# Retention followed by a feed-forward block: another activation, and the second product one chunk behind the first

## The chip, the cores and the metric

The kernel runs on one core of a Trainium2 chip. The time is that of the device for one execution, in microseconds; lower is better.

## What is computed

q, k and v are [8, 8, 576, 64] in float32, w_in [512, 2048] and w_out [2048, 512] in float64.

```python
scores = scale * np.matmul(q, k.transpose(0, 1, 3, 2))
ret = scores * Dmat[None, :, :, :]        # gamma_h ** (i - j) where j <= i, else 0
attn = np.matmul(ret, v)
x = np.ascontiguousarray(attn.transpose(0, 2, 1, 3)).reshape(B * S, H * D)   # [4608, 512]
h = x @ w_in
sp = np.maximum(h, 0.0) + np.log1p(np.exp(-np.abs(h)))                       # softplus
g = h * erf(sp)
out = (g @ w_out).astype(np.float32)
```

## The kernel before

**Retention.** The sequences are cut into 40 pieces of up to 128 tokens of one batch element with all heads (per batch element four of 128 tokens and one of 64). `piece_stages` is a generator with three stages for a piece, written in this order on every engine's queue: the transposes of q and k into PSUM and their copies `qT`, `kT` to SBUF (L222, L224); the scores of the two heads of each pair and their causal mask `sT` (L232, L235); the outputs from `sT` and v, from qT and the running `state`, the product `kv` for the next state, the evacuation of the outputs into `xT` and the state's update (L247 to L291). All PSUM tiles of these stages come from one pool of two buffers, `at`. `load` fetches a piece two ahead, on SP's queue; POOL scales the keys (L208).

**Weights.** They come in float64 and are rounded to float32 on the chip, in 32 parts of 512 weights per partition, two of w_in and two of w_out for a group. `round_weights(g)` does a group's four parts: two ACT operations (L166, L167), five on DVE (L169 to L181), two on POOL (L185, L186), on temporaries `wa`, `wb`, `wr` with two buffers each.

**Feed-forward.** The 4608 tokens are nine chunks of 512, and d_ff is eight groups of two blocks of 128: 72 slots (c, g). A slot's first product (`hidden`, L323) makes `ph`, one PSUM tile per block, which ACT copies to `h` in SBUF (L330). `softplus_terms`, `softplus` and `serf` make g from h: Softplus through Tanh, Abs and Ln, Erf through Gelu and a reciprocal, with a power series for small values, on ACT, DVE and POOL. The second product (`project`, L379) of the group runs two slots later (`LAG`), in four PSUM tiles `po` that collect a chunk's eight groups; ACT copies them out (L388).

**Order.** The schedule is manual: instructions stand on each engine in the order of the program. Four pieces of retention come first, each followed by the four parts of one group; then the loop over slots, in which a slot's two halves of the second product alternate with stages of the retention for the next chunk, and slots 0 to 3 of the first chunk end with four parts of weights each:

```python
        for part in range(2):
            if i >= LAG:
                project(*slots[i - LAG], range(part * NTT // 2, (part + 1) * NTT // 2))
            if now:
                base, goal = stages_for((c + 1) * TCH), stages_for((c + 2) * TCH)
                attend(base + (goal - base) * (2 * g + 1 + part) // (2 * n_g))
```

Of the kernel before, what the change touches and what calls it, by code (L numbers as in the profile page):

```python
# [52 lines left out]
def kernel(  # L53
# [67 lines left out]
    def weight_parts(g):  # L121
# [7 lines left out]
        for ft in range(g * GF, (g + 1) * GF):  # L129
            yield w_out_sb[:, ft : ft + 1, :], w_out[ft * P : (ft + 1) * P, :].rearrange(  # L130
                "(c p) f -> p c f", p=P
            ), slice(0, D_MODEL)

    parts = [(g, *part) for g in range(n_g) for part in weight_parts(g)]
# [311 lines left out]
```

## Time and profile before

| | |
|---|---|
| time, median of 3 runs | 1539.33 us (1535.58 to 1543.75) |
| profiled execution, first to last instruction | 1537.4 us; its time around that is not listed apart, and the median is 1.9 us above the span |
| busy share of the span | DVE 85%, PE 83%, POOL 68%, PE's weight loads 43%, ACT 56% |
| mean granted clock of TensorE | 0.907 of full |
| HBM traffic | 45.68 MB read, 9.44 MB written, 36 GB/s over the span |

A line of a timeline gives the start in us from the first instruction, the duration, the engine, the line of the kernel and the operation, the tiles as output<-input, shapes, how many instructions were merged (x16), and in brackets the idle time of the engine before it with what ended it. The first product's 1152 matmuls are those of two instructions for each matmul of the source. The granted clock is a share of the full 2.4 GHz; the lower level is 0.5. "Busy" of PE is the union of its instructions, so a matmul that runs at the lower clock counts as longer busy.

### The profile page before, as it was taken

Reading aid. Unit: us, or ns where it says so; the run is one execution under the profiler, and the core shown is the slowest. Engines: PE = TensorE matmul, PEld = TensorE weight load, DVE = VectorE, ACT = ScalarE, POOL = GpSimd, SP = SyncE. Lnnn points to the kernel's source line nnn. Section 1 sums busy time; section 2 is a strip of 40 time slices with the busy share of each in tenths; the row PEclk is TensorE's granted clock in tenths of the full one; section 3 lists DMA queues with packets and bytes.
Section 4 is the critical chain, followed back from the end, with each engine's and each line's share of the span. In section 5 each row is a group of like instructions: output and inputs, shape, how many; then the busy total and the mean of one; then the engine's idle time right before and its main releaser. Section 6 shows DMA issues by size and latency. Waiting matters only on the chain.

```text
span 1537.4 us, 12085 instructions
## 1 busy us (share of the span) xinstructions
PE 1281.9 (83%) x4416; PEld 662.0 (43%) x4416; DVE 1299.4 (85%) x853; ACT 858.3 (56%) x893; POOL 1039.7 (68%) x542
## 2 busy tenths in 40 slices
PE   3451454999999899998998999989999999989885
PEld 3330222554444455544444454444444444444332
DVE  5678999887888879888888888898898988888884
ACT  2126443466665556665665666555656665557762
POOL 3346566667776677757766677767777767666774
PEclk7566777999999899999999999999999999999997
DMA  7233220021101210120101110110111110000000
GB/s 191 73 110 89 75 75 14 11 42 48 21 11 21 62 27 12 21 62 8 21 11 48 41 22 29 30 35 9 47 31 35 28 38 1 0 0 27 1 0 28
DMA packets 124556, 55.91 MB, mean 36 GB/s; under 512 B 113616, under 2 KB 113616, under 8 KB 124496
## 3 DMA queue, kind: packets, MB, share of 16 engines
q1 hardware_dynamic: 124352, 54.54, 14.0%
q8 instruction: 35, 0.57, 0.1%
q10 hardware_dynamic: 144, 0.59, 0.1%
q14 instruction: 25, 0.20, 0.0%
HBM read 45.68 MB, written 9.44 MB: 36 GB/s over the span
## 4 chain that ended last, share of the span: by engine, by line
DVE 50%; PE 26%; ACT 16%; issue 5%; POOL 3%; DMA 0%; POOLq 0%; DVEq 0%; ACTq 0%
DVE r L361 18%; PE ph L323 12%; DVE s L353 6%; DVE r L363 6%; DVE r L367 4%; PE o L247 3%; DVE wa L175 3%; PE o L257 3%; DVE wa L172 3%; PE po L379 2%; DVE r L364 2%; PE kv L283 2%; ACT L343 2%; ACT L360 2%; DVE sT L235 2%
## 5 line engine op out<-in xcount | busy, mean ns | idle before, releaser
L379 PE MATMUL po<-w_out_sb,h 128*128 128x512 f32 x1152 | 525.9, 604 | 24.5 <-POOL h L368 24.5
L323 PE MATMUL ph<-xT,w_in_sb 128*128 128x512 f32 x1152 | 525.5, 610 | 6.0 <-ACT h L330 5.4
L361 DVE RECIPROCAL r<-s 128x1024 f32<-128x1024 f32 x72 | 471.8, 6553 | 7.0
L368 POOL TENSOR_TENSOR h<-h,r 128x1024 f32<-128x1024 f32 x72 | 169.7, 2357 | 357.4 <-DVE r L367 325.5
L379 PEld LDWEIGHTS po<-w_out_sb,h 128*128 128x128 f32 x1152 | 218.1, 193 | 290.6 <-issue 256.2
L323 PEld LDWEIGHTS ph<-xT,w_in_sb 128*128 128x128 f32 x1152 | 221.0, 197 | 262.8 <-issue 255.6
L330 ACT COPY h<-ph 128x512 f32<-128x512 f32 x144 | 83.1, 585 | 398.3 <-PE ph L323 398.3
L353 DVE SCALAR_TENSOR_TENSOR s<-h,s 128x1024 f32<-128x1024 f32 x72 | 167.9, 2332 | 49.7 <-ACT s L343 49.7
L346 POOL TENSOR_TENSOR tail<-tail,p 128x1024 f32<-128x1024 f32 x72 | 185.3, 2574 | 6.0
L349 POOL TENSOR_TENSOR tail<-tail,p 128x1024 f32<-128x1024 f32 x72 | 181.5, 2520 | 5.6
L348 POOL TENSOR_TENSOR tail<-tail,p 128x1024 f32<-128x1024 f32 x72 | 177.4, 2463 | 6.0
L247 PE MATMUL o<-sT,raw_v 128*64 128x128 f32 (+1 forms) x640 | 68.3, 327 | 114.2 <-DVE sT L235 113.8
L363 DVE TENSOR_TENSOR r<-r,z 128x1024 f32<-128x1024 f32 x72 | 131.5, 1827 | 8.6 <-ACT z L360 8.6
L232 PE MATMUL s<-qT,kT 64*128 64x128 f32 (+1 forms) x640 | 70.0, 294 | 82.0 <-DVE kT L224 82.0
L166 ACT ACTIVATE wa<-wraw 128x512 f32<-128x512 f32 x32 | 21.5, 672 | 171.3 <-POOL w_in_sb L186 142.4
L247 PEld LDWEIGHTS o<-sT,raw_v 128*64 128x64 f32 (+1 forms) x640 | 49.5, 171 | 151.0 <-DVE sT L235 144.6
L232 PEld LDWEIGHTS s<-qT,kT 64*128 64x128 f32 (+1 forms) x640 | 62.2, 196 | 111.0 <-DVE kT L224 89.8
L339 ACT ACTIVATE p<-h 128x1024 f32<-128x1024 f32 x72 | 76.1, 1057 | 59.0 <-POOL tail L349 58.4
L272 DVE TENSOR_TENSOR xT<-o,cst 128x512 f32<-128x512 f32 (+1 forms) x44 | 25.7, 591 | 90.9 <-PE o L257 82.9
L367 DVE COPY_PREDICATED r<-mask,tail 128x1024 f32<-128x1024 uint8 x72 | 94.7, 1315 | 7.8 <-DVE r L364 0.9
L347 POOL TENSOR_SCALAR tail<-tail 128x1024 f32<-128x1024 f32 x72 | 95.6, 1327 | 6.3
L185 POOL TENSOR_TENSOR wb<-wb,wr 128x512 f32<-128x512 f32 x32 | 41.6, 1301 | 86.0 <-DVE wb L181 86.0
(43 smaller groups left out, 1587.7 us busy)
## 6 DMA issues: line engine op xcount, KB each, us to landing
out_dram<-osb SPq DMA_DIRECT2D x36, 256.0 KB, 2.1
raw_k<-in_k_dram SPq DMA_DIRECT2D x32, 256.0 KB, 3.1
raw_q<-in_q_dram SPq DMA_DIRECT2D x32, 256.0 KB, 4.0
raw_v<-in_v_dram SPq DMA_DIRECT2D x32, 256.0 KB, 4.3
wraw<-in_moe_w_in_dram SPq DMA_DIRECT2D x16, 512.0 KB, 3.4
wraw<-in_moe_w_out_dram SPq DMA_DIRECT2D x16, 512.0 KB, 3.3
raw_k<-in_k_dram SPq DMA_DIRECT2D x8, 128.0 KB, 2.9
raw_q<-in_q_dram SPq DMA_DIRECT2D x8, 128.0 KB, 3.5
```

The source lines that it names most:

```text
L232: nc.tensor.matmul(ps[:n, p, :n], lhsT=T["k"][r, p, :n], rhs=T["q"][r, p, :n], start=True, stop=True)
L247: nc.tensor.matmul(o[e * D : (e + 1) * D, p, :n], lhsT=t["v"][:n, 2 * p + e, :], rhs=sT[:n, e, p, :n], start=(p == 0), stop=(old is None a ...
L323: nc.tensor.matmul(ph, lhsT=w_in_sb[:, dc, f : f + P], rhs=xts[c][:, dc, :], start=(dc == 0), stop=(dc == n_dc - 1),)
L346: nc.gpsimd.tensor_tensor(out=e, in0=e, in1=p2, op=ALU.mult)
L348: nc.gpsimd.tensor_tensor(out=e, in0=e, in1=p2, op=ALU.mult)
L349: nc.gpsimd.tensor_tensor(out=e, in0=e, in1=p, op=ALU.add)
L353: nc.vector.scalar_tensor_tensor(out=s, in0=h, scalar=1e-30, in1=s, op0=ALU.max, op1=ALU.subtract)
L361: nc.vector.reciprocal(out=r, in_=s)
L363: nc.vector.tensor_tensor(out=r, in0=r, in1=z, op=ALU.mult)
L367: nc.vector.copy_predicated(r, m, tail)
L368: nc.gpsimd.tensor_tensor(out=h, in0=h, in1=r, op=ALU.mult)
L379: nc.tensor.matmul(po[tt], lhsT=h[:, j * TCH + tt * P : j * TCH + (tt + 1) * P], rhs=w_out_sb[:, ft, :], start=(ft == 0), stop=(ft == n_ft ...
```

## The change

- *Activation.* `ph` is one PSUM tile of 1024 columns (two buffers) for both blocks. ACT writes Softplus of it to SBUF and then Erf in place, and DVE multiplies by `ph`, read from PSUM. The temporaries, the power series, the reciprocal and POOL's share go, as does the copy of h.
- *Second product one chunk behind.* In chunk c, slot g, the loop has four quarters: first product of block 0, second product, first product of block 1, second product. The second products are those of chunk c - 1, in the order `steps_out`: all eight groups for the first two blocks of 128 tokens, then all eight for the other two. `gpool` has 12 buffers, so that a chunk's eight g stay; the raw weights share them. After the last chunk, eight slots hold second products alone.
- *Staged retention.* The three stages are functions, listed so that a piece's transposes stand between the scores and the outputs of the piece before; a quarter ends with at most one stage. Scores alternate the two heads, each in its own PSUM tile. The copies `qT`, `kT` move from DVE to ACT.
- *Weights.* All of w_in is rounded before w_out, in place: the destination serves as `wa`, the raw words as `wb` and `wr`. Four parts stand ahead of the first slot, one at a time among the stages; the other 28 at the ends of slots 1 to 7 of chunk 0, four each. Four parts are fetched ahead instead of three.

```diff
-    WAHEAD = 3
-    LAG = 2  # slots between a group's first product and its second
+    WAHEAD = 4
...
-    raw = ctx.enter_context(tc.tile_pool(name="raw", bufs=PREFETCH + 1))
+    raw = ctx.enter_context(tc.tile_pool(name="raw", bufs=PREFETCH + 2))
...
-    gpool = ctx.enter_context(tc.tile_pool(name="gpool", bufs=LAG + 2))
...
+    gpool = ctx.enter_context(tc.tile_pool(name="gpool", bufs=12))
...
+    parts = [p for g in range(n_g) for p in parts_in(g)] + [p for g in range(n_g) for p in parts_out(g)]
+    N_IN = len(parts) // 2
...
+                t_f = gpool.tile([P, W], FP32, tag="g", name="wraw")
...
+            r_f, high_f = pairs_f[:, :, :, 0], pairs_f[:, :, :, 1]
+            a_f, a = dst, dst.bitcast(UINT32)
             nc.scalar.activation(a_f, high_f, AF.Abs)
             nc.scalar.mul(out=r_f, in_=low, mul=2.0**-52)
...
+            nc.vector.tensor_scalar(out=high, in0=a, scalar1=0xFF800000, scalar2=None, op0=ALU.bitwise_and)
+            nc.gpsimd.tensor_tensor(out=r_f, in0=high_f, in1=r_f, op=ALU.mult)
+            nc.gpsimd.tensor_tensor(out=a_f, in0=a_f, in1=r_f, op=ALU.add)
             load_weights()
...
-            T[name] = att.tile([P, NP, P], FP32, tag=name + "T", name=name + "T")
-            nc.vector.tensor_copy(out=T[name][:, :, :n], in_=pt[:, :, :n])
...
+            t[name + "T"] = att.tile([P, NP, P], FP32, tag=name + "T", name=name + "T")
+            nc.scalar.copy(out=t[name + "T"][:, :, :n], in_=pt[:, :, :n])
...
+    def scores(i):
+        n, t = pieces[i][2], live[i]
+        sT = t["sT"] = att.tile([P, 2, NP, P], FP32, tag="sT", name="sT")
+        ps = [ps_at.tile([P, NP, P], FP32, tag="at", name=f"s{e}") for e in range(2)]
+        for p in range(NP):
+            for e in range(2):
+                r = slice(e * D, (e + 1) * D)
+                nc.tensor.matmul(
+                    ps[e][:n, p, :n], lhsT=t["kT"][r, p, :n], rhs=t["qT"][r, p, :n], start=True, stop=True
+                )
...
+    stages = [(transposes, 0)]
+    for i in range(len(pieces)):
+        stages.append((scores, i))
+        if i + 1 < len(pieces):
+            stages.append((transposes, i + 1))
+        stages.append((outputs, i))
...
+    def serf(c, g, ph):
+        t = gs_of[c, g] = gpool.tile([P, W], FP32, tag="g", name="g")
+        nc.scalar.activation(t, ph, AF.Softplus)
+        nc.scalar.activation(t, t, AF.Erf)
+        nc.vector.tensor_tensor(out=t, in0=ph, in1=t, op=ALU.mult)
...
+    steps_out = [(half, g) for half in range(2) for g in range(n_g)]
...
+    need = stages_for(TCH)
+    for n in range(need):
+        attend(n + 1)
+        round_weights(1 + (N_IN // n_g + 1) * (n + 1) // need)
+    QUARTERS = 4
+    for c in range(n_ch + 1):
+        for g in range(n_g):
+            if c < n_ch:
+                ph = ps_h.tile([P, W], FP32, tag="ph", name="ph")
+                base, goal = stages_for((c + 1) * TCH), stages_for(min((c + 2) * TCH, n_tok))
+            for part in range(QUARTERS):
+                if c < n_ch and part % 2 == 0:
+                    hidden(c, g, [part // 2], ph)
+                    if part == 2:
+                        serf(c, g, ph)
+                elif c > 0 and part % 2 == 1:
+                    project(c - 1, 2 * g + part // 2)
+                if c < n_ch:
+                    attend(base + (goal - base) * (QUARTERS * g + part + 1) // (QUARTERS * n_g))
+            if c == 0:
+                round_weights(N_IN // n_g * (g + 2) + N_IN * g // n_g)
+            if c == 1:
+                round_weights(len(parts))
```

PE in a slot of the main loop, before (`ph` is the first product, `po` the second, `pt` transposes, `s` scores):

```order
L323 MATMUL ph<-xT,w_in_sb 128x512 x8
L379 MATMUL po_834<-w_out_sb,h 128x512 x2
L379 MATMUL po_837<-w_out_sb,h 128x512 x2
L232 MATMUL s_1363<-qT,kT 128x128 x4
L232 MATMUL s_1369<-qT,kT 128x128 x4
L379 MATMUL po_861<-w_out_sb,h 128x512 x2
L379 MATMUL po_864<-w_out_sb,h 128x512 x2
L247 MATMUL o<-sT,raw_v 64x128 x8
```

and PE in a slot of chunk 1 of the changed kernel:

```order
L308 MATMUL ph<-xT,w_in_sb 128x512 x4
L334 MATMUL po_1078<-w_out_sb,g 128x512 x2
L334 MATMUL po_1081<-w_out_sb,g 128x512 x2
L205 MATMUL pt_q<-ident,raw_q 128x128 x4
L205 MATMUL pt_k<-ident,raw_k 128x128 x4
L308 MATMUL ph<-xT,w_in_sb 128x512 x4
L334 MATMUL po_1078<-w_out_sb,g 128x512 x2
L334 MATMUL po_1081<-w_out_sb,g 128x512 x2
L234 MATMUL o<-sT,raw_v 64x128 x8
L270 MATMUL kv<-raw_v,raw_k 128x128 x4
```

The first product is cut in two and the second lies between; where scores and outputs stood one half of a second product apart, stages now stand two groups apart or more.

DVE from the end of slot 2's rounding to slot 3's in chunk 0 of the changed kernel (`g<-ph,g` is the multiply, L159 to L170 a part of the rounding):

```order
L170 TENSOR_SCALAR wraw<-w_in_sb 128x512
L259 TENSOR_TENSOR xT<-o,cst 128x4x128
L275 TENSOR_TENSOR state<-kv,cst 128x512
L320 TENSOR_TENSOR g<-ph,g 128x1024
L220 TENSOR_TENSOR sT<-s_640,cst 128x512
L220 TENSOR_TENSOR sT<-s_641,cst 128x512
L159 TENSOR_SCALAR w_in_sb<-w_in_sb 128x2x256
L162 TENSOR_SCALAR w_in_sb<-w_in_sb 128x2x256
```

The evacuations that free `at` and `ph` stand behind a whole burst of four parts; before, they stood behind the reciprocal as well.

ACT at slot 7 of chunk 0 of the changed kernel, with the waits (Pool, DVE, PE and DMAHW name the engine or DMA queue waited for):

```order
L156 ACTIVATE w_out_sb<-wraw 128x512 [waits DMAHW5_49]
L157 ACTIVATE wraw<-wraw 128x512
L207 COPY qT<-pt_q 128x4x64 [waits PE_49]
L207 COPY kT<-pt_k 128x4x64 [waits PE_49]
L318 ACT_TABLE_LOAD [waits DVE_49,PE_49]
L318 ACTIVATE g<-ph 128x1024 [waits Pool_49]
L319 ACT_TABLE_LOAD
L319 ACTIVATE g<-g 128x1024 [waits Activation_49]
```

Softplus writes to a buffer that raw weights had, and so waits for POOL's last read of them; in slot 7 this is the last part of slot 6's burst.

## Rows read from the trace of the kernel before

**Rows 1.** The page: busy us (share of the span) and instructions by engine.

```profile
PE 1281.9 (83%) x4416; PEld 662.0 (43%) x4416; DVE 1299.4 (85%) x853; ACT 858.3 (56%) x893; POOL 1039.7 (68%) x542
```

**Rows 2.** The page: the chain that ended last, shares by engine.

```profile
DVE 50%; PE 26%; ACT 16%; issue 5%; POOL 3%; DMA 0%; POOLq 0%; DVEq 0%; ACTq 0%
```

**Rows 3.** Windows: stretch, length, busy by engine, granted clock, DMA share, GB/s.

```profile
0.00:99.30 99.30, 40.56 (x216) 35.02 (x217) 61.42 (x86) 18.51 (x29) 37.08 (x35) 0.64 0.49 129
99.30:274.50 175.20, 81.53 (x283) 43.37 (x282) 158.25 (x142) 73.76 (x89) 109.45 (x69) 0.71 0.22 65
274.50:1523.20 1248.70, 1149.65 (x3906) 579.58 (x3904) 1079.68 (x625) 763.65 (x771) 893.12 (x439) 0.96 0.10 25
```

**Rows 4.** Timeline of PE in two slots of the main stretch.

```profile
1110.97 7.03 PE L323 MATMUL ph<-xT,w_in_sb 128*128 128x512 f32 x16
1117.84 3.60 PE L379 MATMUL po<-w_out_sb,h 128*128 128x512 f32 x8
1121.27 0.60 PE L222 MATMUL pt_q<-ident,raw_q 128*128 128x128 f32 x4
...
1122.15 3.60 PE L379 MATMUL po<-w_out_sb,h 128*128 128x512 f32 x8
1127.13 1.71 PE L232 MATMUL s<-qT,kT 64*128 64x128 f32 x16 [1.39 <-DVE kT L224]
1128.78 7.13 PE L323 MATMUL ph<-xT,w_in_sb 128*128 128x512 f32 x16
...
1139.27 1.09 PE L247 MATMUL o<-sT,raw_v 128*64 128x128 f32 x16
1140.30 1.16 PE L257 MATMUL o<-qT,state 128*128 128x128 f32 x8
1141.29 1.06 PE L283 MATMUL kv<-raw_v,raw_k 128*128 128x128 f32 x8
1142.18 3.60 PE L379 MATMUL po<-w_out_sb,h 128*128 128x512 f32 x8
```

**Rows 5.** Groups by line on ACT: busy us, mean ns, idle before.

```profile
L339 ACT ACT_TABLE_LOAD x72 | 92.4, 1283 | 1.3
L330 ACT COPY h<-ph 128x512 f32<-128x512 f32 x144 | 83.1, 585 | 398.3 <-PE ph L323 398.3
L360 ACT ACTIVATE z<-s 128x1024 f32<-128x1024 f32 x72 | 76.1, 1057 | 0.9
L166 ACT ACTIVATE wa<-wraw 128x512 f32<-128x512 f32 x32 | 21.5, 672 | 171.3 <-POOL w_in_sb L186 142.4 <-POOL w_out_sb L186 18.3 <-DMA wraw<-in_moe_w_in_dram 10.4
```

**Rows 6.** Groups by line on DVE: the state's add, with kv in PSUM.

```profile
L290 DVE TENSOR_TENSOR state<-kv,state 128x512 f32<-128x512 f32 x24 | 16.6, 690 | 9.1 <-PE kv L283 8.7
```

**Rows 7.** Timeline of PE near the end, after a gap.

```profile
1473.88 8.83 PE L379 MATMUL po<-w_out_sb,h 128*128 128x512 f32 x16 [2.48 <-POOL h L368]
```

**Rows 8.** Timeline of ACT at the end: the last copy of the output.

```profile
1533.72 0.60 ACT L388 ACTIVATE osb<-po 128x512 f32<-128x512 f32 x1 [1.40 <-PE po L379]
```

**Rows 9.** Timeline of DVE and POOL in the second burst of rounding.

```profile
45.75 0.42 DVE L169 TENSOR_SCALAR wa<-wa 128x512 f32<-128x512 f32 x1
...
48.42 1.31 POOL L185 TENSOR_TENSOR wb<-wb,wr 128x512 f32<-128x512 f32 x1 [11.11 <-DVE wb L181]
48.65 1.37 DVE L172 TENSOR_SCALAR wa<-wa 128x512 uint32<-128x512 uint32 x1
...
50.05 1.63 DVE L175 SCALAR_TENSOR_TENSOR wa<-wraw,wa 128x512 uint32<-128x512 uint32 x1
...
60.83 0.43 DVE L181 TENSOR_SCALAR wb<-wa 128x512 uint32<-128x512 uint32 x1
```

**Rows 10.** Timeline of PE before the first slot: the scores of two pieces.

```profile
62.51 3.09 PE L232 MATMUL s<-qT,kT 64*128 64x128 f32 x16 [16.63 <-DVE kT L224]
...
90.14 3.09 PE L232 MATMUL s<-qT,kT 64*128 64x128 f32 x16 [16.63 <-DVE kT L224]
```

**Rows 11.** Windows, the second product's instructions alone, main stretch.

```profile
274.50:1523.20 1248.70, 494.07 (x1088) 205.21 (x1088) 0.96 0.10 25
```

More of the change, by code (lines that the diff above doesn't have):

```diff
@@ L106, in load @@
         loaded[i] = t
-    for i in range(PREFETCH):
-        load(i)
+    load(0)
     cst = const.tile([P, CONST_COLS], FP32, name="cst")
@@ L116, with parts_in, parts_out @@
     tri = cst[:, H + 2 * NP * P : CONST_COLS]
+    for i in range(1, PREFETCH):
+        load(i)
     w_in_sb = const.tile([P, n_dc, D_FF], FP32, name="w_in_sb")
     w_out_sb = const.tile([P, n_ft, D_MODEL], FP32, name="w_out_sb")
-    def weight_parts(g):
+    def parts_in(g):
         f = g * GF * P
-        for dc in range(0, n_dc, WP // (GF * P)):
-            dcs = slice(dc, dc + WP // (GF * P))
-            yield w_in_sb[:, dcs, f : f + GF * P], w_in[dcs.start * P : dcs.stop * P, :].rearrange(
-                "(c p) f -> p c f", p=P
-            ), slice(f, f + GF * P)
+        step = WP // (GF * P)
+        for dc in range(0, n_dc, step):
+            src = w_in[dc * P : (dc + step) * P, :].rearrange("(c p) f -> p c f", p=P)
+            yield w_in_sb[:, dc : dc + step, f : f + GF * P], src, slice(f, f + GF * P)
+    def parts_out(g):
         for ft in range(g * GF, (g + 1) * GF):
[L130 to L134, printed above, removed]
+            src = w_out[ft * P : (ft + 1) * P, :].rearrange("(c p) f -> p c f", p=P)
+            yield w_out_sb[:, ft : ft + 1, :], src, slice(0, D_MODEL)
+    parts = [p for g in range(n_g) for p in parts_in(g)] + [p for g in range(n_g) for p in parts_out(g)]
+    N_IN = len(parts) // 2
     words = []
+    rounded = [0]
     def load_weights():
         if len(words) < len(parts):
-            _, dst, src, cols = parts[len(words)]
+            dst, src, cols = parts[len(words)]
             t = None
@@ L193 @@
     make_identity(nc, ident)
-    half = const.tile([P, 1], FP32, name="half")
-    nc.vector.memset(half, 0.5)
     xts = {}
+    live = {}
     state = {"prev": None}
@@ L210, in weigh_keys, with transposes @@
             )
-    def piece_stages(i):
-        b, s0, n = pieces[i]
-        t = loaded.pop(i)
+    def transposes(i):
+        n = pieces[i][2]
+        t = live[i] = loaded.pop(i)
         load(i + PREFETCH)
         weigh_keys(i + 1)
-        T = {}
         for name in "qk":
@@ L240, in piece_stages, with outputs @@
             )
-        yield
+    def outputs(i):
+        b, s0, n = pieces[i]
+        t = live.pop(i)
         old = state["prev"] if s0 > 0 else None
@@ L292, in piece_stages, with hidden @@
             state["prev"] = new
-        yield
-    def attention():
-        weigh_keys(0)
-        for i in range(len(pieces)):
-            yield from piece_stages(i)
-    att_run = attention()
-    STAGES = 3
+    stages = [(transposes, 0)]
[4 more added lines that the diff above has]
+        stages.append((outputs, i))
     done = [0]
     def stages_for(tokens):
-        return STAGES * sum(1 for b, s0, _ in pieces if b * S + s0 < tokens)
+        last = max(i for i, (b, s0, _) in enumerate(pieces) if b * S + s0 < tokens)
+        return stages.index((outputs, last)) + 1
     def attend(upto):
-        while done[0] < upto:
-            next(att_run)
+        while done[0] < min(upto, len(stages)):
+            of, i = stages[done[0]]
+            of(i)
             done[0] += 1
-    W = GF * TCH
-    tiles = {}
-    def hidden(c, g):
-        t = tiles[c, g] = {"h": gpool.tile([P, W], FP32, tag="h", name="h")}
-        for j in range(GF):
-            ph = ps_h.tile([P, TCH], FP32, tag="ph", name="ph")
+    gs_of = {}
+    def hidden(c, g, js, ph):
+        for j in js:
             f = (g * GF + j) * P
@@ L323, in hidden @@
                 nc.tensor.matmul(
-                    ph,
+                    ph[:, j * TCH : (j + 1) * TCH],
                     lhsT=w_in_sb[:, dc, f : f + P],
@@ L370, with project @@
-    po = {}
-    def project(c, g, tts):
-        h = tiles[c, g]["h"]
-        for tt in tts:
+    def serf(c, g, ph):
[3 more added lines that the diff above has]
+        nc.vector.tensor_tensor(out=t, in0=ph, in1=t, op=ALU.mult)
+    po = {}
+    steps_out = [(half, g) for half in range(2) for g in range(n_g)]
+    def project(c, step):
+        half, g = steps_out[step]
+        t = gs_of[c, g]
+        for tt in (2 * half, 2 * half + 1):
```

117 lines of the change are left out of this document (17 added, 100 removed).

## Prediction

> **What bounds the kernel now.** I read the page's busy shares first: DVE 85%, PE 83% [rows 1], so the shares alone do not say which engine bounds. The chain that ended last does: 50% of the span runs over DVE, 26% over PE, 16% over ACT [rows 2]. Then I cut the span into stretches at PE's landmarks and asked for each engine's busy time [rows 3]. Up to the first `ph` matmul at 99.3 us PE is busy 40.6 of 99.3 us. Up to 274.5 us (the start of slot 4 of chunk 0, when all weights are rounded) it is busy 81.5 of 175.2 us, and DVE 158.3. After that come 1248.7 us in which PE is busy 1149.7: 99 us of idle. So the two early stretches, 274.5 us, leave PE idle 152 us, and the main one is already near PE's limit.
>
> The PE timeline at two full slots gives the prices [rows 4]. Sixteen `ph` instructions (eight matmuls of the source, each two instructions) start at 1110.97 and the `po` ones at 1117.84: 6.88 us at the full granted clock, 430 ns each. Eight `po` take 3.44 us (1117.84 to 1121.27), so a slot's two products take 13.76. One 128-token piece of the retention adds transposes 0.88 (1121.27 to 1122.15), scores 1.65 (1127.13 to 1128.78), outputs with the state and kv 2.91 (1139.27 to 1142.18): 5.44 us. The slot from 1110.97 to 1128.78 is 17.81 us; its products, transposes and scores make 16.29, and the one wait shown is 1.39 for a copy on DVE. The main stretch averages 1248.7 / 68 = 18.4 us a slot; part of that is idle, part the granted clock of 0.96 [rows 3].
>
> **The change, part by part.**
>
> *The activation.* Per slot ACT had two copies of h, three table loads and six functions, DVE a reciprocal and five more operations, POOL six. Now ACT has two table loads of 1.28 and two functions, DVE one multiply, POOL nothing. No row shows Softplus or Erf. Gelu over 128x1024 took 1.06 us and a table load 1.28 [rows 5], so I take 2 x 1.28 + 2 x 1.06 = 4.7 us a slot. DVE's multiply reads PSUM and one SBUF operand as the state's add of 512 columns does, 0.69 us [rows 6]; twice the columns is at most 1.4, and I take 1.2. Nothing of this is on PE's path: `ph` has two buffers, and one is wanted again only after the other's slot, 13.8 us later, against 4.7 + 1.2 = 5.9. The cover is PE's own work of that slot. Nor does PE wait for `g`: the second product runs a whole chunk behind. So from chunk 1 on I cost the activation at nothing, and all 99 us of idle in the main stretch goes.
>
> *Main stretch.* Chunks 1 to 8 have 64 slots with both products: 64 x 13.76 = 880.6 us. Of the 40 pieces, 24 full ones (six of them first in their sequence, without the 0.99 us of `o<-qT,state`) and seven of 64 tokens still come here: 24 x 5.44 - 6 x 0.99 = 124.6, and the small ones at about 2.2 (no kv, half the columns: an estimate) 15.4: 140 us. In PE's order the stages are now two or three groups of matmuls apart, so the transposes' copies, moved to ACT (0.6 each, behind 4.7 of activation), and the masks on DVE have over 6.9 us, and I charge no wait. The scores alternate two heads on separate halves of the array's rows. Outputs, which alternate two halves of its columns, take 1.03 us for 16 instructions where scores take 1.65 [rows 4]. So scores cost between 1.0 and 1.65; I keep 1.65, the row of the same operation, and hold 24 x 0.6 = 15 us as the lower end. The Trainium skill, *TensorE: Matmul & The Clock Gate*, Part 3 (packing small matmuls), says that matmuls on distinct row groups run concurrently; by it scores would halve to 0.83, and the sum would be about 20 us less.
>
> *Last chunk.* Eight slots of second product alone, 8 x 6.88 = 55 us, now with all of `g` ready. Before, groups near the end waited for POOL, and 16 instructions after a gap of 2.48 took 8.83 us where 7.0 is usual [rows 7, 4]. Then the last `osb` copy (0.60) and its DMA: the span of 1537.4 ended 3.7 us after that copy's start [rows 8], so 4.
>
> *Up to the first `ph`.* Before, four pieces went through one after the other with 4 parts rounded between: a burst ran on DVE from 45.75 to 61.26 us, 15.5 us [rows 9], and scores followed scores after 27.63 us [rows 10]. Three bursts stood ahead of the first `ph`. Now three single parts are rounded among the stages. Without the bursts 99.3 - 46.5 = 53 us are left; the first mask now waits for part 0's five DVE operations, 3 us, but transposes and copies run ahead of their piece, and PE, no longer idle for 16.6 us at a time, may hold its full clock (0.64 on average there [rows 3]; scores took 3.09 at the lower level, 1.71 at the upper [rows 10, 4]). Bounds 44 and 58; I take 52.
>
> *Chunk 0.* The other 28 parts go into its slots 1 to 7, four at the end of each, while PE has only 6.88 us a slot: here DVE bounds. A burst is 15.5 us whatever ACT does, because from the second part on DVE's second and third operation take 1.37 and 1.63 (0.42 for the first, before POOL starts) [rows 9]: they end with POOL's two on the part before. Step by step from the first `ph`: two slots of first product 13.8, small stages 2, activation and multiply 5.9: 22 us; six bursts, 93; then what lies between bursts. Slot 2's first product waits for POOL's second part, 9.4 us into burst 1; from there half a block 1.7, scores 1.7, the other block 3.4, activation and multiply 5.9 make 22 us, 25 with part of it at the lower clock: 9.4 behind the burst. Slots 3 to 6 have 4, 3, 2 and 5 operations of 0.69 (masks, x^T, state), a multiply of 1.2 each, and in slots 3 and 6 one or two us until scores are there: 5.0, 3.3, 2.6, 6.6. In slot 7 Softplus waits for POOL's last part of burst 6 (the excerpt of ACT, above), since it takes over that part's buffer: 2.6 of POOL, 4.6 to the end of the multiply, 0.8 of x^T: 8. Sum 22 + 93 + 9.4 + 17.5 + 8 = 150. Then chunk 1 begins; burst 7 runs beside its products. Raw loads queue on SP behind weight loads that wait for a buffer, but are two pieces ahead, so I charge nothing.
>
> What no row shows is POOL's and DVE's price with every second word as an operand (the pairs are now worked on in place). ACT reads them so already, at 0.67 against 0.59 for a copy of the same size [rows 5]. Below nothing is excluded, since the operations are the same; the upper end is POOL at double, 1.31 more [rows 9] on the first, both of whose operands are such, and half of that on the second: 2.0 us x 24 parts ahead of chunk 1 = 48, with DVE's last operation at 0.69 instead of 0.43 6 more. I take nothing, as on ACT, and keep 54 as the upper end. The Trainium skill, *GPSIMD Engine Reference*, section 7, states half as much again for reads whose step is over 8 bytes. The step here is two words, exactly 8, so by it the sum stands; past that step the first operation would add, as an estimate, 0.65 x 24 = 16 us.
>
> **Sum**: 52 + 150 + 880.6 + 140 + 55 + 4 = 1282 us of span. The profiled execution spanned 1537.4 and the median of the runs shown is 1539.33, 2 us above. I forecast **1284 us**.
>
> **Rivals.**
> 1. *Rounding in place costs more* (above): 1284 + 54 = 1338 at the end, about 1314 in the middle. For it: nothing in the rows has POOL on such operands. Against: ACT's row. 18%.
> 2. *PE's clock or small waits stay*: in the main stretch 1088 instructions of the second product were 494.1 us busy [rows 11] where 430 ns each make 467.8: 26 us lost to the clock, and twice that with the first product. If a wait per slot remains that keeps 0.96, 1284 + 52 = 1336. For it: every gap of 2.5 us was followed by slow matmuls [rows 7]. Against: I find nothing left to wait for. 12%.
> 3. *The change doesn't do what it says; PE's idle moves*: stages split into quarters could wait for ACT's copies behind the activation as they waited for DVE's. If a slot stays at 18.4 us, 52 + 150 + 64 x 18.4 + 55 + 6 = 1441. For it: PE's wait of 1.39 was for such a copy [rows 4]. Against: two groups of slack. 5%.
> 4. *Slower: Softplus or Erf takes several passes.* With h held in PSUM, ACT could come to bound a slot. 1539 is reached where a slot takes 16 + 255 / 64 = 20 us: ACT's copies are 0.9 and its loads 2.6, so Softplus and Erf would have to take 16.5 us together, eight times the 2.1 assumed; at 18 a slot is 21.5 and the total 1284 + 64 x 5.5 = 1636. Against: every function of this kernel runs at the rate of a copy [rows 5]. 2%.
>
> **Chances.** The forecast has 63%, with a range of its own from 1262 (scores at 1.0, first `ph` at 44) to 1305 (first `ph` at 58, a dozen us of small waits in chunk 0); the rivals have 18, 12, 5 and 2. For 8 in 10 the range takes in the forecast and most of rivals 1 and 2: 1260 to 1338. A difference under 0.5% (8 us) could not be told from none by runs that spread over 8 us; faster by more than that come all cases but the last and its border: faster 0.97, same 0.01, slower 0.02.
>
> **What would show it.** In the changed profile: the first `ph` near 52 us; the first `po` near 207; 28 parts in bursts of about 15.5 us on DVE; slots of 16.0 us with PE over 97% busy and the clock at 1.00 between; Softplus and Erf at 1.06 with 1.28 before each; and 16 score instructions in 1.0 or in 1.65 us. I am wrong if a slot after chunk 1 shows PE waiting for ACT or DVE, or if bursts take over 18 us.

## The result, and the profile after

The changed kernel takes 1273.33 us (median of 4 runs, 1272.30 to 1274.46), the kernel before 1539.23 in the same session: a ratio of 0.8277, 95% interval 0.8258 to 0.8297. The forecast was 1284 with a range from 1260 to 1338.

The page of the changed kernel answers to [rows 1] and [rows 2]: busy time of each engine, and the chain that ended last.

```profile
PE 1199.3 (94%) x4416; PEld 601.2 (47%) x4416; DVE 305.2 (24%) x412; ACT 429.8 (34%) x469; POOL 121.0 (10%) x110
...
PE 85%; DVE 6%; ACT 1%; issue 0%; DMA 0%; POOL 0%; DVEq 0%; ACTq 0%; POOLq 0%
```

DVE went from 1299 to 305 us and from 50% of the chain to 6%; most of the 6% are the bursts of rounding in chunk 0 (lines L162 and L165 of the chain). PE's busy time fell too, from 1282 to 1199, though it executes the same 4416 instructions: they run at a higher granted clock, and the scores are shorter. The windows are cut at the first `ph`, the first of chunk 1 and the start of the last chunk's second products; columns as in [rows 3].

```profile
0.00:46.30 46.30, 29.71 (x225) 24.86 (x226) 18.36 (x32) 12.63 (x20) 14.73 (x18) 0.93 0.98 226
46.30:188.70 142.40, 91.29 (x394) 49.15 (x392) 111.17 (x156) 69.72 (x93) 66.20 (x55) 0.82 0.40 115
188.70:1212.50 1023.80, 1023.06 (x3672) 502.92 (x3672) 174.61 (x225) 344.34 (x352) 40.03 (x37) 1.00 0.11 27
1212.50:1272.30 59.80, 55.20 (x128) 24.24 (x128) 1.07 (x1) 3.12 (x6) 0.00 (x0) 0.99 0.07 27
```

The third row is the main result: in 1023.8 us PE is busy 1023.1, at a granted clock of 1.00 (2.4 GHz), where the kernel before was busy 1149.7 of 1248.7 us at 0.96 [rows 3] (a stretch with 3906 of its instructions; here it is 3672). Of the 73 us that PE is still idle, 51 lie in the second row and 17 in the first. PE's timeline shows the start of chunk 1, then its second and third slot, then the start of the last chunk with both products and, in the last row, the second product of the last chunk.

```profile
188.74 5.58 PE L308 MATMUL ph<-xT,w_in_sb 128*128 128x512 f32 x8 [10.93 <-DVE xT L259]
194.16 3.60 PE L334 MATMUL po<-w_out_sb,g 128*128 128x512 f32 x8
...
205.26 3.60 PE L308 MATMUL ph<-xT,w_in_sb 128*128 128x512 f32 x8
208.70 3.60 PE L334 MATMUL po<-w_out_sb,g 128*128 128x512 f32 x8
212.13 0.60 PE L205 MATMUL pt_q<-ident,raw_q 128*128 128x128 f32 x4
212.57 0.60 PE L205 MATMUL pt_k<-ident,raw_k 128*128 128x128 f32 x4
213.00 3.60 PE L308 MATMUL ph<-xT,w_in_sb 128*128 128x512 f32 x8
216.44 3.60 PE L334 MATMUL po<-w_out_sb,g 128*128 128x512 f32 x8
219.97 0.68 PE L234 MATMUL o<-sT,raw_v 64*64 64x64 f32 x16
220.58 1.10 PE L244 MATMUL o<-qT,state 128*128 128x64 f32 x8
221.52 3.65 PE L308 MATMUL ph<-xT,w_in_sb 128*128 128x512 f32 x8
225.01 3.60 PE L334 MATMUL po<-w_out_sb,g 128*128 128x512 f32 x8
228.44 3.60 PE L308 MATMUL ph<-xT,w_in_sb 128*128 128x512 f32 x8
231.97 1.16 PE L216 MATMUL s<-qT,kT 64*128 64x128 f32 x16
233.06 3.70 PE L334 MATMUL po<-w_out_sb,g 128*128 128x512 f32 x8
236.60 3.60 PE L308 MATMUL ph<-xT,w_in_sb 128*128 128x512 f32 x8
...
1102.19 3.70 PE L308 MATMUL ph<-xT,w_in_sb 128*128 128x512 f32 x8 [0.52 <-DVE xT L259]
...
1212.85 55.20 PE L334 MATMUL po<-w_out_sb,g 128*128 128x512 f32 x128 [0.52 <-ACT osb L343]
```

No bracket stands behind a row of the two slots: PE waits for nothing there. In the whole main stretch PE is idle 0.7 us, and 0.52 of it is the one wait at 1102.19, for the x^T that its chunk begins with. A group of eight takes 3.43 from start to start (225.01 to 228.44), before and behind transposes as well (208.70 to 212.13, 213.00 to 216.44). Before outputs or scores it takes 3.53 (216.44 to 219.97, 228.44 to 231.97), and a group right behind scores takes 3.54 (233.06 to 236.60). Sixteen scores take 1.09 us (231.97 to 233.06).

On ACT and DVE the new activation costs what was forecast (groups by line; busy us, mean ns, idle before):

```profile
L319 ACT ACT_TABLE_LOAD x72 | 92.4, 1283 | 1.3
L319 ACT ACTIVATE g<-g 128x1024 f32<-128x1024 f32 x72 | 76.1, 1056 | 0.8
L318 ACT ACTIVATE g<-ph 128x1024 f32<-128x1024 f32 x72 | 73.8, 1024 | 491.2 <-PE ph L308 487.4 <-POOL w_out_sb L172 3.8
```
```profile
L320 DVE TENSOR_TENSOR g<-ph,g 128x1024 f32<-128x1024 f32 x72 | 88.2, 1224 | 762.4 <-ACT g L319 623.1 <-PE po L334 139.2
```

### The profile page after: what moved, and what is told of

The parts are those of the page before. It is cut to its first block, busy times and chain, and to the rows that moved or that the text cites. A ratio compares the mean times of both kernels' runs of the same rounds, so it can differ in the third digit from the quotient of the medians.

```text
span 1272.3 us, 10583 instructions
## 1 busy us (share of the span) xinstructions
PE 1199.3 (94%) x4416; PEld 601.2 (47%) x4416; DVE 305.2 (24%) x412; ACT 429.8 (34%) x469; POOL 121.0 (10%) x110
## 4 chain that ended last, share of the span: by engine, by line
PE 85%; DVE 6%; ACT 1%; issue 0%; DMA 0%; POOL 0%; DVEq 0%; ACTq 0%; POOLq 0%
PE po L334 39%; PE ph L308 35%; PE s L216 3%; PE o L234 2%; PE o L244 2%; PE kv L270 2%; DVE w_out_sb L165 1%; PE pt_q L205 1%; PE pt_k L205 1%; DVE w_in_sb L165 1%; DVE w_out_sb L162 1%; DVE w_in_sb L162 1%; DMA wraw<-in_moe_w_out_dram 0%; DVE wraw L170 0%; DVE w_out_sb L159 0%
## 5 line engine op out<-in xcount | busy, mean ns | idle before, releaser
L334 PE MATMUL po<-w_out_sb,g 128*128 128x512 f32 x1152 | 518.2, 595 | 0.5 <-ACT osb L343 0.5
L334 PEld LDWEIGHTS po<-w_out_sb,g 128*128 128x128 f32 x1152 | 215.7, 190 | 260.9 <-issue 256.9
L320 DVE TENSOR_TENSOR g<-ph,g 128x1024 f32<-128x1024 f32 x72 | 88.2, 1224 | 762.4 <-ACT g L319 623.1
L318 ACT ACTIVATE g<-ph 128x1024 f32<-128x1024 f32 x72 | 73.8, 1024 | 491.2 <-PE ph L308 487.4
L193 POOL TENSOR_TENSOR raw_k<-raw_k,cst 128x512 f32<-128x512 f32 (+1 forms) x40 | 42.7, 1071 | 746.7 <-DMA raw_k<-in_k_dram 746.7
L207 ACT COPY qT<-pt_q 128x512 f32<-128x512 f32 (+1 forms) x40 | 21.6, 541 | 216.1 <-PE pt_q L205 216.1
L319 ACT ACTIVATE g<-g 128x1024 f32<-128x1024 f32 x72 | 76.1, 1056 | 0.8
L220 DVE TENSOR_TENSOR sT<-s,cst 128x512 f32<-128x512 f32 (+1 forms) x80 | 46.9, 627 | 46.4 <-PE s L216 46.4
L171 POOL TENSOR_TENSOR wraw<-wraw 128x512 f32<-128x512 f32 x32 | 34.4, 1076 | 107.2 <-issue 61.4
L234 PE MATMUL o<-sT,raw_v 128*64 128x128 f32 (+1 forms) x640 | 42.2, 275 | 1.1 <-ACT qT L207 1.0
L244 PE MATMUL o<-qT,state 128*128 128x128 f32 (+1 forms) x256 | 37.6, 291 | 0.0
```

Of the source, the lines that this page charges most:

```text
L171: nc.gpsimd.tensor_tensor(out=r_f, in0=high_f, in1=r_f, op=ALU.mult)
L193: nc.gpsimd.tensor_tensor(out=t[:n], in0=t[:n], in1=gk[:n].unsqueeze(2).to_broadcast([n, H, D]), op=ALU.mult)
L220: nc.vector.tensor_tensor(out=sT[:n, e, :, :n], in0=ps[e][:n, :, :n], in1=tri[:n, :n].unsqueeze(1).to_broadcast([n, NP, n]), op=ALU.mult,)
L234: nc.tensor.matmul(o[e * D : (e + 1) * D, p, :n], lhsT=t["v"][:n, 2 * p + e, :], rhs=t["sT"][:n, e, p, :n], start=(p == 0), stop=(old is N ...
L244: nc.tensor.matmul(o[:, p, :n], lhsT=old[:, p, :], rhs=t["qT"][:, p, :n], start=False, stop=(p == NP - 1), skip_group_check=True,)
L318: nc.scalar.activation(t, ph, AF.Softplus)
```

## Experiments

Ten more kernels ran. Each is compared with runs of the kernel before on the same chip; differences to the changed kernel below go by its 1273.33 us. They ask what each half of the change is worth, what covers the activation, and what bounds the early stretches.

### The activation alone

The kernel before, with only this in the place of `softplus_terms`, `softplus` and the old `serf` (and a factor of 1 in the output copies):

```diff
+        nc.scalar.activation(s, h, AF.Softplus)
+        nc.scalar.activation(s, s, AF.Erf)
+        nc.vector.tensor_tensor(out=h, in0=h, in1=s, op=ALU.mult)
```

> The kernel before with the new activation alone: Softplus and Erf on ACT from h in SBUF and one multiply on DVE, in place of the six functions, DVE's six operations and POOL's. Order, lag of two slots, PSUM tiles and rounding stay. Theory (the end is set by PE once DVE no longer has 13.9 us of activation in each slot; the new order is worth the early stretches and the waits around the stages only): up to the first ph 99.3 us as before; slots 0 to 3 lose 4 x 12.7 = 51 us of DVE work at most, 124 to 175 us; the main stretch loses its 99 us of idle and about half or all of 52 us of low clock, 1098 to 1125 us; 1323 to 1400 us in all, 1330 the likeliest. Rival (the order carries the gain): PE still waits in each slot for a copy or a mask between two stages of the same piece, about 2 us with the low clock behind it, and the main stretch stays over 1200 us: 1430 us or more.

Measured: 1317.99 us, ratio 0.8579 (0.8565 to 0.8593). So the activation alone brings 219 of the 266 us (1537.25 before on that chip). Its windows, cut at the first `ph`, at slot 4 and at the end:

```profile
0.00:97.26 97.26, 38.57 (x216) 32.87 (x217) 61.42 (x86) 18.55 (x29) 37.08 (x35) 0.68 0.52 132
97.26:182.53 85.27, 58.54 (x203) 30.38 (x201) 73.42 (x97) 37.06 (x52) 47.62 (x35) 0.82 0.46 125
182.53:1315.90 1133.37, 1125.86 (x4001) 563.64 (x4000) 230.02 (x310) 424.87 (x453) 44.68 (x41) 1.00 0.12 29
```

From slot 4 on PE is busy 1125.9 of 1133.4 us at the full clock, in the old order with its lag of two slots. The waits between two stages of a piece were not the order's: with DVE free, the copies and masks come in time but for 3 us in all. The rival falls. What is left for the new order is 45 us. The stretch of slots 0 to 3 came out at 85, below my 124 to 175. I had taken 51 us of activation off DVE, but its busy time there fell by 85 (158.3 [rows 3] to 73.4). The rounding on it fell too, from 100 us for 20 parts to 63 for 16: the last four parts now lie behind the start of slot 4, and a part takes 4.0 us instead of 5.0. Why a part is shorter was not run apart.

### The order alone

The other half: the changed kernel with the old activation behind each `ph`.

```diff
-        nc.scalar.activation(t, ph, AF.Softplus)
-        nc.scalar.activation(t, t, AF.Erf)
-        nc.vector.tensor_tensor(out=t, in0=ph, in1=t, op=ALU.mult)
+        nc.scalar.copy(out=h, in_=ph)
+        nc.scalar.activation(s, h, AF.Tanh, scale=0.5)
...
+        nc.vector.reciprocal(out=r, in_=s)
...
+        nc.gpsimd.tensor_tensor(out=h, in0=h, in1=r, op=ALU.mult)
...
```

> The changed kernel with the activation of before: ACT copies ph to h in SBUF, then the six functions, POOL's five operations and DVE's six follow in one piece, on single-buffered temporaries; three raw buffers instead of four. Order, second product one chunk behind, rounding and PSUM tiles as changed. Theory (the two halves of the change need each other: the order puts each x^T, mask and state behind the activation of its slot on DVE, and the chunk's last x^T behind 13.9 us of DVE work and ACT's chain): PE waits some 15 to 20 us at each of eight chunk ends and a few us at stages between, chunk 0 gets 8 x 12.7 us more on DVE: 1450 to 1600 us. Rival (the parts add up: the activation alone brought 1318 from 1537, so the order is worth 45 us on its own): 1490 within 10 by the sum, which only tells apart if it is missed. Rival 2 (DVE's 15 us fit into PE's 16 and nothing waits from chunk 1 on): 1273 + 101 in chunk 0, 1375 us.

Measured: 2031.4 us, ratio 1.3211 (1.3189 to 1.3233), far over all three. The timeline of one slot (DVE and PE):

```profile
1015.23 6.55 DVE L344 RECIPROCAL r<-s 128x1024 f32<-128x1024 f32 x1
...
1025.48 0.68 DVE L264 TENSOR_TENSOR xT<-o,cst 128x512 f32<-128x512 f32 x1
...
1026.21 2.67 PE L221 MATMUL s<-qT,kT 64*128 64x128 f32 x16 [11.33 <-DVE xT L264]
```

PE waits for `at`, which an x^T behind the whole activation on DVE frees: 222 us of PE's waits end with a mask, 287 with an x^T, 85 with an output copy on ACT (L374), 49 with a `qT`; the clock falls to 0.82. My theory named the place and charged it mainly at the chunk ends; it is at stages all along, 31 waits for a mask and 26 for an x^T. So this order pays only with a short activation. How much of the loss is due to my writing the activation in one piece, rather than staggered over two slots as before, was not tried.

### The activation twice

```diff
         nc.scalar.activation(t, ph, AF.Softplus)
         nc.scalar.activation(t, t, AF.Erf)
+        nc.scalar.activation(t, ph, AF.Softplus)
+        nc.scalar.activation(t, t, AF.Erf)
```

> The changed kernel with Softplus and Erf computed twice in every slot, the second pair overwriting the first (the output is the same): ACT has two more table loads of 1.28 and two more functions of 1.04, 4.7 us a slot. Theory (from chunk 1 on the activation is covered by PE's 16 us a slot): the main stretch stays at 1024 us within 3; in chunk 0 one to three of the eight slots have the activation on the path, +5 to +14; 1278 to 1288 us. Rival (the activation or a wait behind it is on PE's path from chunk 1 on): 64 x 4.7 = 300 us more, 1574 us; if only a wait for qT or kT behind it appears, 31 pieces x 1 to 2 us, 1305 to 1335 us.

Measured: 1373.4 us, ratio 0.8935 (0.8917 to 0.8953): +100, which neither theory gave. In chunk 0 the stretch grows from 142.4 to 171.0 us. 28.6 / 4.7 would put the activation on the path in about six slots there, not in one to three (at most: 6 us of the growth are PE's own busy time, at a granted clock of 0.77 for 0.82). The main stretch grows from 1023.8 to 1094.2. There 48 us are PE's waits: 27.3 in seven waits of 3.3 to 4.7 us for the x^T that a new chunk begins with, 11.9 for output copies behind the activation on ACT, 8.5 for masks and `qT`. The end of one chunk, on all engines (rows in order of time):

```profile
495.61 1.06 ACT L321 ACTIVATE g<-g 128x1024 f32<-128x1024 f32 x1
496.57 1.05 ACT L345 COPY osb<-po 128x512 f32<-128x512 f32 x2
496.70 1.22 DVE L322 TENSOR_TENSOR g<-ph,g 128x1024 f32<-128x1024 f32 x1 [13.48 <-ACT g L321]
...
497.84 0.74 DVE L259 TENSOR_TENSOR xT<-o,cst 128x256 f32<-128x256 f32 x2
...
498.31 4.12 PE L308 MATMUL ph<-xT,w_in_sb 128*128 128x512 f32 x6 [3.33 <-DVE xT L259]
```

The last x^T of a chunk stands behind that slot's multiply on DVE, and so behind the activation. With 4.7 us less of it the wait of 3.33 would be 1.4 us of slack, and the longest of the seven, 4.69, none: the activation's cover at a chunk's end is 0 to 1.4 us (an estimate from these waits). The changed kernel itself is that close. At the end of its chunk 6 the x^T stands right behind the multiply and is done at 973.67, 0.03 us before PE's next first product at 973.70:

```profile
971.78 1.22 DVE L320 TENSOR_TENSOR g<-ph,g 128x1024 f32<-128x1024 f32 x1 [13.48 <-PE po L334]
972.92 0.75 DVE L259 TENSOR_TENSOR xT<-o,cst 128x256 f32<-128x256 f32 x2
```

After such a wait in the doubled run eight matmuls take 5.2 us instead of 3.43 (498.31 to the next group at 503.55), at a granted clock of 0.67; the seven together lose some 14 us to it.

### Scores head after head

```diff
-        for p in range(NP):
-            for e in range(2):
+        for e in range(2):
+            for p in range(NP):
```

> The changed kernel with the scores written head after head: four matmuls on the upper half of the array's rows, then four on the lower, instead of alternating. Theory (alternating halves lets neighbours overlap: 16 instructions take 1.09 us in the changed kernel, 1.65 in the order of before): 16 instructions take 1.5 to 1.65 us again, in 31 of the 40 pieces on PE's path, 24 x 0.56 and 7 x 0.2 to 0.3 more: +13 to +16 us, 1286 to 1290. Rival (scores are shorter because PE arrives at them warm and without a wait, whatever their order): 1.09 us stays and the time is 1273 within 2.

Measured: 1288.35 us, ratio 0.8384 (0.8370 to 0.8398): +15.0, as the theory had it. Sixteen scores take 1.64 us again:

```profile
331.63 1.71 PE L216 MATMUL s<-qT,kT 64*128 64x128 f32 x16
333.27 3.70 PE L334 MATMUL po<-w_out_sb,g 128*128 128x512 f32 x8
```

So the rival falls, and the order of these two loops is worth 15 of the order's 45 us.

### Weights by group again

```diff
-    parts = [p for g in range(n_g) for p in parts_in(g)] + [p for g in range(n_g) for p in parts_out(g)]
+    parts = [p for g in range(n_g) for f in (parts_in, parts_out) for p in f(g)]
...
-        round_weights(1 + (N_IN // n_g + 1) * (n + 1) // need)
+        round_weights(16 * (n + 1) // need)
...
-                round_weights(N_IN // n_g * (g + 2) + N_IN * g // n_g)
+                round_weights(16 + 4 * (g + 1))
```

> The changed kernel with the weights rounded group after group as before the change: the four parts of four groups, 16 parts, among the stages ahead of the first slot, the other 16 at the ends of slots 0 to 3; all else as changed. Theory (what counts is how much rounding stands where PE has nothing beside it; w_in first lets the first product start after 4 parts): 12 more parts at 3.7 us ahead of the first ph, which comes at 91 us instead of 46.3; chunk 0 then has 16 parts instead of 28 and lasts about 117 us instead of 142; first product of chunk 1 at 208 us instead of 188.7: +19, 1288 to 1298 us. Rival (DVE's 32 parts bound either way, and the order of the parts is worth nothing): 1273 within 4.

Measured: 1289.42 us, ratio 0.8378 (0.8364 to 0.8392): +16. The first `ph` comes at 79.0, the first of chunk 1 at 203.8 (windows of this kernel):

```profile
0.00:79.02 79.02, 36.50 (x225) 31.28 (x225) 62.87 (x88) 25.33 (x43) 41.80 (x39) 0.74 0.83 233
79.02:203.81 124.79, 91.82 (x393) 49.62 (x393) 88.55 (x121) 60.13 (x74) 53.43 (x45) 0.86 0.29 71
```

Each side was 8 to 12 us off, in opposite directions: part of the rounding ahead of the first slot fits into DVE's idle time there (16 us are left of 28), and chunk 0 keeps its waits from stage to stage (PE is idle for 33 of its 124.8 us). With the scores, this makes 31 of the order's 45 us. I did not look for the other 14 by a run of their own.

### One buffer more

```diff
-    gpool = ctx.enter_context(tc.tile_pool(name="gpool", bufs=12))
+    gpool = ctx.enter_context(tc.tile_pool(name="gpool", bufs=13))
```

> The changed kernel with 13 buffers for g and the raw weights in place of 12. Theory (in slot 7 of chunk 0 Softplus waits until POOL has left the last part of burst 6, since it takes over that part's buffer; 7.65 us lie between the end of burst 6 on DVE and the next first product): Softplus runs during burst 6, the multiply starts at its end, the next ph follows about 2 us after: -5.7 us, 1267.5. Rival (DVE or POOL is late there for another reason, or the wait shows up at the next slot): the gap stays above 6 us and the time at 1273 within 2.

Measured: 1271.14 us, ratio 0.8271 (0.8258 to 0.8283), which the runs do not tell from the changed kernel's 0.8277. The trace does: the first `ph` of chunk 1 comes at 185.06 instead of 188.74. The wait has moved by one part, not gone. Softplus in slot 7, first of the changed kernel, then of this one:

```profile
183.65 1.02 ACT L318 ACTIVATE g<-ph 128x1024 f32<-128x1024 f32 x1 [1.18 <-POOL w_out_sb L172]
```
```profile
179.97 1.02 ACT L318 ACTIVATE g<-ph 128x1024 f32<-128x1024 f32 x1 [1.29 <-POOL w_out_sb L172]
```

Buffers are handed on in turn, so one more puts Softplus behind the part before the last: 3.7 us earlier, one part, where I had 5.7.

### Rounding on temporaries again

```diff
-            a_f, a = dst, dst.bitcast(UINT32)
+            a_f = wtmp.tile(shape, FP32, tag="wa", name="wa")[:, :, :]
+            b_f = wtmp.tile(shape, FP32, tag="wb", name="wb")[:, :, :]
+            r_f = wtmp.tile(shape, FP32, tag="wr", name="wr")[:, :, :]
...
-            nc.gpsimd.tensor_tensor(out=r_f, in0=high_f, in1=r_f, op=ALU.mult)
+            nc.gpsimd.tensor_tensor(out=b_f, in0=b_f, in1=r_f, op=ALU.mult)
...
```

> The changed kernel with the rounding on temporaries again (wa, wb, wr, two buffers each, as in the kernel before), all else as changed. Theory (POOL's first operation is shorter in place, 1.08 us against 1.30, although both of its operands have a step of two words, and a burst is set by POOL's two operations together): POOL's first operation takes 1.30 again, four parts 15.5 us on DVE instead of 14.9, six bursts ahead of chunk 1: +3 to +5 us, 1276 to 1278. Rival (the shorter 1.08 comes from what else runs then, not from the operands): 1.08 and 14.9 stay, 1273 within 2. Other side (in place costs elsewhere, as ACT's or DVE's reads of every second word): under 1271.

Measured: 1274.36 us, ratio 0.8286 (0.8274 to 0.8298): not told apart by time. POOL's first operation, in this kernel and in the changed one (groups by line):

```profile
L176 POOL TENSOR_TENSOR wb<-wb,wr 128x512 f32<-128x512 f32 x32 | 41.6, 1299 | 103.0 <-DVE wb L175 101.4 <-ACT qT L212 1.6
```
```profile
L171 POOL TENSOR_TENSOR wraw<-wraw 128x512 f32<-128x512 f32 x32 | 34.4, 1076 | 107.2 <-issue 61.4 <-DVE wraw L170 24.2 <-ACT w_in_sb L156 6.6
```

So the 1.08 us belong to the operands. Both forms write on one of their inputs, so it is not the place of the output; in the changed kernel both inputs are every second word of the raw tile, here they are contiguous. A burst takes 15.5 us again (68.56 to 84.09) for 14.9 in the changed kernel (67.84 to 82.75), and six of them 93.2 for 90.4; against that, Softplus in slot 7 no longer waits for POOL, since the raw words are done with earlier (the gap between burst 6 and the next `ph` is 5.5 us instead of 7.65). The first `ph` of chunk 1 is 0.9 us later.

### Rounding without POOL

```diff
-            nc.gpsimd.tensor_tensor(out=r_f, in0=high_f, in1=r_f, op=ALU.mult)
-            nc.gpsimd.tensor_tensor(out=a_f, in0=a_f, in1=r_f, op=ALU.add)
+            nc.vector.tensor_tensor(out=r_f, in0=high_f, in1=r_f, op=ALU.mult)
+            nc.vector.tensor_tensor(out=a_f, in0=a_f, in1=r_f, op=ALU.add)
```

> The changed kernel with the two operations of the rounding that POOL does given to DVE, which then does all seven of a part. Theory (while POOL works, DVE's own operations are held up by about what POOL takes: 0.43 becomes 1.15 and 0.69 becomes 1.65, so that POOL's share saves DVE nothing): without POOL they take 0.43 and 0.69 in every part, the two added ones 0.69 each, a part 3.8 us where it takes 3.73 now, four parts 15.1; the buffer in slot 7 comes free 2.6 us earlier: 1269 to 1276 us. Rival (1.15 and 1.65 have another cause and stay): a part takes 5.1 us, six bursts 33 us more, 1306 us.

Measured: 1281.91 us, ratio 0.8334 (0.8319 to 0.8348): +8.6, over the theory's range and far under the rival's. The second part of a burst in the changed kernel, on POOL and on DVE, then on DVE in this one:

```profile
70.52 1.09 POOL L171 TENSOR_TENSOR wraw<-wraw 128x512 f32<-128x512 f32 x1 [16.63 <-DVE wraw L170]
71.68 1.34 POOL L172 TENSOR_TENSOR w_in_sb<-w_in_sb,wraw 128x512 f32<-128x512 f32 x1
```
```profile
70.74 1.15 DVE L162 TENSOR_SCALAR w_in_sb<-w_in_sb 128x512 uint32<-128x512 uint32 x1
71.92 1.65 DVE L165 SCALAR_TENSOR_TENSOR w_in_sb<-wraw,w_in_sb 128x512 uint32<-128x512 uint32 x1
...
74.86 1.15 DVE L162 TENSOR_SCALAR w_in_sb<-w_in_sb 128x512 uint32<-128x512 uint32 x1
```
```profile
77.83 0.43 DVE L162 TENSOR_SCALAR w_in_sb<-w_in_sb 128x512 uint32<-128x512 uint32 x1
78.29 0.69 DVE L165 SCALAR_TENSOR_TENSOR w_in_sb<-wraw,w_in_sb 128x512 uint32<-128x512 uint32 x1
...
81.81 0.43 DVE L162 TENSOR_SCALAR w_in_sb<-w_in_sb 128x512 uint32<-128x512 uint32 x1
```

Without POOL DVE's two operations take 0.43 and 0.69, as the theory said; with it each ends 0.3 to 0.6 us after POOL's. A part takes 3.99 us (four from 73.41 to 89.38) where it takes 3.73 with POOL, the gaps between dependent operations included, which I had left out. Six bursts take 97.3 us for 90.4; chunk 0 as a whole grows by 2 only, since the gaps behind the first and the sixth burst shrink from 7.5 and 7.65 to 3.8 and 6.4. Ahead of the first slot, where parts stand singly and POOL's work holds up little on DVE, its share did help: without it the first `ph` comes at 51.75 instead of 46.29. So POOL's 2.4 us of work a part save DVE 0.26 in the mean of a burst, and that is all from its first part, beside which POOL has no part to work on: it takes 2.4 us. From the second part on a part takes 4.12 with POOL (70.74 to 74.86) and 3.98 without (77.83 to 81.81). The Trainium skill, *SBUF — State Buffer*, section "SBUF: two separate sides", says that some DVE operations, those with two SBUF inputs among them, and GpSimd's exclude each other from a shared port for a whole instruction; the rows above agree.

### w_out just in time

The 28 later parts singly, at the ends of quarters: two a slot in slots 0 to 5 of chunk 0, three from slot 6 on into chunk 1; and 15 buffers.

```diff
-    gpool = ctx.enter_context(tc.tile_pool(name="gpool", bufs=12))
+    gpool = ctx.enter_context(tc.tile_pool(name="gpool", bufs=15))
...
+    ROUND = {(0, g, q) for g in range(6) for q in (1, 3)}
+    ROUND |= {(c, g, q) for c, g in ((0, 6), (0, 7), (1, 0), (1, 1), (1, 2)) for q in (0, 1, 3)}
+    ROUND |= {(1, 3, 0)}
...
+                if (c, g, part) in ROUND:
+                    round_weights(rounded[0] + 1)
-            if c == 0:
-                round_weights(N_IN // n_g * (g + 2) + N_IN * g // n_g)
-            if c == 1:
-                round_weights(len(parts))
```

> The changed kernel with the 28 later parts spread out: one part at the ends of single quarters of the slots instead of four at the end of a slot (two parts a slot in slots 0 to 5 of chunk 0, three in slots 6 and 7 and in slots 0 to 2 of chunk 1, the last in slot 3), so that w_out is rounded just ahead of its use in chunk 1, and 15 buffers for g and raw weights instead of 12. Theory (in chunk 0 the six bursts ahead of chunk 1 bound; 10 parts of 3.7 us go behind the start of chunk 1, beside PE's full slots, and PE no longer waits 5 to 11 us at a time for a burst to end): chunk 0 142 to 105 us, 1230 to 1245 us in all. Rival 1 (the second product of chunk 1 waits for w_out: a part there takes DVE and POOL 4 us and three stand in a slot of 16, with masks, x^T and the multiply behind them): 10 to 25 us of waits in chunk 1, 1250 to 1265. Rival 2 (chunk 0 is not bounded by the bursts but by the chain stage after stage): 1270 or more.

Measured: **1226.74 us**, ratio 0.7976 (0.7962 to 0.7991), 46.6 us under the changed kernel and the fastest of all. Chunk 0 and the main stretch:

```profile
46.71:141.82 95.11, 80.37 (x395) 43.31 (x393) 81.45 (x121) 62.48 (x79) 48.84 (x41) 0.98 0.45 130
141.82:1165.00 1023.18, 1022.66 (x3672) 503.40 (x3672) 197.91 (x259) 350.18 (x362) 58.03 (x52) 1.00 0.13 30
```

Chunk 0 falls from 142.4 to 95.1 us, 10 under the forecast 105; the clock, which I had not counted, comes along (0.82 to 0.98: PE's same work is 80.4 us busy instead of 91.3). Six parts fewer ahead of chunk 1 (18 for 24 after the first `ph`) would be 22 us at 3.73; the rest I put down to the spreading, which lets PE's groups and the stages run between single parts. These two and the three more buffers were not run apart (one buffer more, alone, brought 3.7 us in the trace above). The ten parts that stand in chunk 1 cost nothing: PE is busy 1022.7 of 1023.2 us there. Both rivals fall.

### The same without POOL

> The kernel with the weights spread out and 15 buffers (1226.7 us), with POOL's two operations of the rounding given to DVE as well. Theory (POOL's share saves DVE nothing, and the hand-over from DVE to POOL goes): a part takes DVE 3.8 us where it took about 3.7, single parts end 2 to 3 us earlier for whoever waits for the weights: 1222 to 1229 us. Rival (a single part lets POOL work while DVE does something else, masks and multiplies that it does not hold up): 18 parts x 1.4 us more on DVE in chunk 0, 1240 to 1252.

The edit to that kernel, and the second POOL line likewise:

```diff
-            nc.gpsimd.tensor_tensor(out=r_f, in0=high_f, in1=r_f, op=ALU.mult)
+            nc.vector.tensor_tensor(out=r_f, in0=high_f, in1=r_f, op=ALU.mult)
...
```

Measured: 1232.69 us, ratio 0.8017 (0.8003 to 0.8031), +6.0 and between theory and rival. In the traces the first `ph` comes 2.2 us later (48.95 for 46.71) and chunk 0 is 2.5 us longer (97.6 for 95.1). So with single parts POOL's work does save DVE something; that it lies beside idle time of DVE is my reading of it.

## Why the prediction was right

The forecast was 10.7 us too high, from the stretch up to the first `ph` and from chunk 0. The profile answers term by term:

- **First `ph`**: 46.3 for 52, near the lower bound 44. PE held a granted clock of 0.93 where it had 0.64 [rows 3]; the step had named this and taken the middle.
- **Chunk 0**: 142.4 for 150. The first burst began after 21.6 us (22), six bursts made 90.4 (93), and behind them lay 7.5 (9.4), 15.4 (17.5) and 7.65 (8). The bursts are shorter because rounding on the raw words costs less, not more, as the run on temporaries shows (1.08 us on POOL instead of 1.31 [rows 9]). Here a step failed: "Below nothing is excluded, since the operations are the same". The same operations on other operands were faster. Rival 1 falls. The Trainium skill's rule for it (*GPSIMD Engine Reference*, section 7) sets in past 8 bytes and was not reached here; it does not tell of a gain.
- **Main stretch**: 1023.8 for 1020.6, and so close by luck: two errors of opposite sign. Scores took 1.09, not the 1.65 that I kept: the bounds of 1.0 and 1.65 were right, the choice of the "row of the same operation" was the mis-sized term, 24 x 0.56 = 13.4 us. Against it stands what I left out of 13.76 a slot: a group of eight before or behind scores or before outputs takes 0.1 us more (3.53 or 3.54 for 3.43, above), three times a piece, so about 10 us over 31 pieces (an estimate from these rows); the small pieces took 2.8 instead of 2.2 (outputs 0.61 and 0.94 in the rows above), 4 us; and the group at 188.74, the first after a wait, took 5.42 for 3.43. *TensorE: Matmul & The Clock Gate*, Part 3 of the Trainium skill, was right that distinct row groups overlap; the halving to 0.83 that the prediction worked out from it did not come, the rows show 1.09.
- **Last chunk and tail**: 59.8 for 59.
- **The activation at nothing**: right in the sum, wrong in its cover. The step set 5.9 us against 13.8 of a whole slot. The step left out the x^T behind the multiply. The run with the activation doubled shows the real cover, 0 to 1.4 us at a chunk's end. Had Softplus and Erf taken twice as long, 2.1 us more, the forecast would have missed a wait of about 0.7 to 2.1 us at each chunk's end (an estimate from those waits). By the prediction's own sign, a slot after chunk 1 in which PE waits for DVE, it is wrong in one place: the 0.52 us at 1102.19, where the x^T itself waits 0.43 us for the outputs that PE finished just before.
- **Rivals 2 to 4**: the clock is 1.00 and PE is idle 0.7 us in the main stretch; a slot takes 1023.8 / 64 = 16.0 us, not 18.4; Softplus takes 1.02 and Erf 1.06.

## What to carry to other kernels

Where a slow engine's chain stands behind everything, shorten that chain first: 219 of 266 us came from it, the old order then ran almost without waits, and the new order with the old chain, written in one piece, was 32% slower than before. When a cost is set at nothing because something covers it, look for the place where the cover is shortest (here the end of a chunk, 0 to 1.4 us), not at the average slot. One-off work belongs, in small portions, where the bounding engine is full and the worker idle: ten parts of rounding beside chunk 1's full slots cost PE nothing, and with the others spread singly chunk 0 was 47 us shorter.
